# Shared PSUM banks, seven chained products for three input blocks, joint last-query scores, and an order written out by hand

## The chip, the core and the metric

The kernel runs on one core of a Trainium2 chip. Its time is the device time of one execution in microseconds (us). The engines are named as in the profile: PE does matrix products (PEld is its weight load), ACT applies functions, DVE does elementwise work, POOL starts loads, SP starts stores and transposing DMAs. PE writes its results to PSUM, eight banks of 128 partitions x 512 fp32 numbers; ACT and DVE read them there. Each engine runs its own queue in order and waits where a value isn't there yet.

## The reference

Attention with a relative position bias (8 batches, 8 heads, 576 positions, 64 numbers per head), and then two dense layers on its result:

```python
scores = scale * np.matmul(q, k.transpose(0, 1, 3, 2))
scores = scores + bias.transpose(2, 0, 1)[None, :, :, :]   # bias_table[bucket(|i - j|)]
attn = np.exp(scores - np.max(scores, axis=-1, keepdims=True))
attn = attn / (np.sum(attn, axis=-1, keepdims=True) + 1e-09)
out = np.matmul(attn, v)
...
x = np.ascontiguousarray(out.transpose(0, 2, 1, 3)).reshape(B * S, H * D)   # 4608 x 512
h = x @ w_in                                                                # 512 x 2048
g = np.maximum(0.01 * h, h)
return (g @ w_out).astype(np.float32)                                       # 2048 x 512
```

## The kernel before

**Attention.** The 8 heads of a batch make four pairs; `n` counts the 32 pairs. For a pair, q and k are loaded (POOL), copied next to each other by DVE (`rows`, buffer `pr`, three of them), transposed by a DMA on SP's queue (`turn_by_dma`, buffer `tu`) and copied into `qt` and `kt` (`take_turned`). The scores of a pair are six units: u = 0 to 3 are 128 keys each against queries 0 to 511, one product for each head, which stand in the two halves of PE's rows (64x128 tiles) and run at the same time; u = 4 is queries 512 to 575 (the "last queries") of both heads against 4 x 128 keys, with `apart` having put the two heads' queries side by side with zeros between, in the full 128x128 tile; u = 5 is the last 64 keys. ACT takes the exponent of each (`expo`), DVE multiplies the five blocks by the bias's exponent (`band`), PE multiplies by v (`av`, `av_tail`), whose 65th column gives the sum, DVE divides head by head (`norm`), and the result is transposed into `xT` by a DMA (`x_dma`).

**Dense layers.** 512 positions make a tile T, of which there are nine. `ffn_in` makes 16 blocks h of 128 x 512, each from four products of 512 columns (L556), ACT applies the leaky ReLU (`ffn_act`, L560). The second layer is done with seven block products in place of eight (`product`, L604): DVE makes four sums of blocks of g first (`mix_g`, L582), each product has its own PSUM bank, and DVE adds the seven up in `y` (`combine`, L617). `mix_weights` makes the sums of weights once.

**PSUM.** The eight banks are shared out by use: two double banks for scores (S), one bank (O), three banks (M) for everything else.

**Order.** Nothing is scheduled by the compiler. Class `Plan` lists all steps with an estimated cost, what they come after and what PSUM they take, and makes each engine's queue by a list scheduler with ranks, shifted by a table (`SHIFT`, `HOLD`, `SWAP`). Where it expects PE to be idle in the first 26 us it puts in filling products (`spin`, L879). The first layer can't start before the first batch's attention is done, since all four pairs make up the 512 columns of x; from then on the products of the dense layers stand between the attention steps, and after the last pair they run alone.

Of the kernel before, what the change touches and what calls it, by code (L numbers as in the profile page):

```python
# [36 lines left out]
class Plan:  # L37


    LAG, COLD, WARM, EARLY, PATIENCE = 0.25, 4.9, 26.0, 34.0, 0.3  # L40

    SHIFT = {
# [12 lines left out]
    }  # L55

    HOLD = {
        2: 19.6, 15: 64.2, 20: 6.9, 31: 13.4, 33: 28.9, 38: 9.6, 40: 11.1, 43: 25.5, 208: 57, 1127: 179.7,
    }

    SWAP = (62, 63, 88, 91, 117, 184, 212, 261, 269, 270, 952, 1141,)

    def __init__(self, slots):
        self.tasks = []
        self.slots = {k: [0.0] * v for k, v in slots.items()}
        self.slots["M"][-1] = self.WARM

    def add(self, engine, cost, after, go, rank, take=(), give=(), tail=0.0, at=None):
        t = {"engine": engine, "cost": cost, "after": list(after), "go": go, "rank": rank, "n": len(self.tasks),
             "take": list(take), "give": list(give), "tail": tail, "end": at, "start": at}  # L70
        if at is None:
            self.tasks.append(t)
        return t

    def link(self, ins):

        for t in self.tasks:
            t["after"] = [ins[d[1:]] if isinstance(d, tuple) else d for d in t["after"]]
            t["behind"] = [d for d in t["after"] if d["engine"] == t["engine"] == "POOL"]
            t["after"] = [d for d in t["after"] if not any(d is o for o in t["behind"])]  # L80

    def order(self):

        for t in self.tasks:
            t["rank"] += self.SHIFT.get(t["n"], 0)
            if t["n"] in self.SWAP:
                t["engine"], t["cost"] = t["other"]
        free, done, waiting, ring = {}, [], {}, 0.0
        slots = {k: list(v) for k, v in self.slots.items()}
        for t in self.tasks:  # L90
            waiting.setdefault(t["engine"], []).append(t)
        while any(waiting.values()):
            best = None
            for e, ts in waiting.items():
                now = free.get(e, 0.0)
                ready = []
                for t in ts:
# [5 lines left out]
                    for k in set(t["take"]):  # L103
                        s, m = sorted(self.slots[k]), t["take"].count(k)
                        r = max(r, s[m - 1]) if len(s) >= m else None
                        if r is None:
                            break
# [53 lines left out]
def kernel(  # L161
# [10 lines left out]
    nc = tc.nc  # L172
# [741 lines left out]
```

## Time and profile before

| | us |
|---|---|
| time, three runs | 367.48, 367.71, 370.26 (median 367.71) |
| profiled execution: its span, first to last instruction | 367.0 |
| PE busy | 355.8 |
| DVE busy | 266.8 |
| ACT busy | 246.5 |
| first product of the dense layers starts (L556) | 33.13 |
| last product ends | 362.09 |

The profile holds the span of its execution alone; the median of the runs is 0.7 us above it, which is what this text takes for what lies around a span. A product's row in the trace lasts longer than the engine is taken by it, since products overlap: what PE can do is read from the starts of products that follow each other. A row with "x8" is eight instructions, from the first's start to the last's end. The chain of waits names, from the last instruction backwards, what each step waited for. The idle time before an instruction is put down to what ended it.

### The profile page before, as it was taken

What the parts mean: (1) busy time and instruction counts of PE and PEld (TensorE: products, weight loads), DVE (VectorE), ACT (ScalarE), POOL (GpSimd) and SP (SyncE); (2) the same over time, 40 slices, a digit from 0 to 9 for tenths busy, and PEclk for the clock granted to TensorE, in tenths of its full rate; (3) what the DMA queues carried; (4) which work ended last, traced back from release to release, by engine and by line L of the source; (5) the groups of instructions that cost most, each with busy time, mean ns of one, the idle gap of its engine ahead of it and who ended that gap; (6) DMA issues with size and microseconds to landing.
All of it is one profiled execution on the core that took longest, in us unless ns stands there. A gap on an engine that the chain in (4) does not pass through costs nothing.

```text
span 367.0 us, 9617 instructions
## 1 busy us (share of the span) xinstructions
PE 355.8 (97%) x4022; PEld 239.7 (65%) x4022; DVE 266.8 (73%) x650; ACT 246.5 (67%) x356; POOL 71.8 (20%) x107
## 2 busy tenths in 40 slices
PE   8999999799999999999999999999999999999994
PEld 6666556575587556865678788656875587445883
DVE  6997799598799679975997779757984384320482
ACT  5998998558955897579857885797568911565000
POOL 8955122082007100700052005000000000000000
PEclk9999999999999999999999999999999999999999
DMA  8999999999919993999189929932222110300033
GB/s 128 153 182 196 204 180 154 134 81 191 215 20 89 192 162 73 118 205 170 20 86 197 156 71 89 116 53 72 82 21 75 20 59 2 114 0 2 1 116 114
DMA packets 103163, 39.56 MB, mean 108 GB/s; under 512 B 83152, under 2 KB 97488, under 8 KB 103120
## 3 DMA queue, kind: packets, MB, share of 16 engines
q0 software_dynamic: 53424, 18.21, 48.5%
q1 hardware_dynamic: 49488, 20.46, 30.6%
q8 instruction: 31, 0.51, 0.6%
q10 hardware_dynamic: 208, 0.29, 0.3%
q14 instruction: 12, 0.10, 0.1%
HBM read 36.70 MB, written 9.44 MB: 126 GB/s over the span
## 4 chain that ended last, share of the span: by engine, by line
PE 87%; DVE 5%; ACT 3%; DMA 3%; issue 1%; ACTq 0%
PE pm L556 32%; PE pm L604 28%; PE ps_s L437 8%; PE ps_om L506 5%; PE ps_o L506 5%; DMA tu<-pr 3%; ACT at L451 2%; PE ps_s L441 2%; PE ps_s L444 2%; PE ps_w L879 2%; DVE at L471 1%; PE ps_o L491 1%; DVE sum L582 1%; PE ps_tx L533 1%; DVE opair L519 0%
## 5 line engine op out<-in xcount | busy, mean ns | idle before, releaser
L451 ACT ACTIVATE at<-ps_s 128x1024 bf16<-128x1024 f32 x124 | 121.0, 1027 | 27.4 <-PE ps_s L437 27.3
L556 PE MATMUL pm<-xT,w_in_sb 128*128 128x512 bf16 (+1 forms) x640 | 134.1, 358 | 0.0
L560 ACT ACTIVATE gt<-pm 128x512 bf16<-128x512 f32 x144 | 84.7, 604 | 50.1 <-PE pm L556 48.4
L556 PEld LDWEIGHTS <-w_in_sb 128*128 128x128 bf16 x640 | 59.1, 98 | 57.1 <-issue 5.1
L471 DVE TENSOR_TENSOR at<-at,hk 128x768 bf16<-128x768 bf16 (+4 forms) x156 | 67.1, 448 | 30.6 <-ACT at L451 22.6
L604 PEld LDWEIGHTS <-gt 128*128 128x128 bf16 x576 | 54.6, 98 | 10.8 <-issue 3.6
L249 POOL DMA_DIRECT2D vn<-in_v_dram x32 | 30.2, 954 | 145.2 <-PE ps_o L506 130.0
L617 DVE TENSOR_TENSOR y<-pm,y 128x512 f32<-128x512 f32 (+1 forms) x54 | 41.9, 775 | 20.8 <-PE pm L604 19.3
L604 PEld LDWEIGHTS <-sum 128*128 128x128 bf16 x432 | 41.3, 98 | 9.6 <-issue 2.5
L506 PEld LDWEIGHTS <-at 128*128 128x128 bf16 x1240 | 41.1, 98 | 4.0 <-issue 1.2
L437 PE MATMUL ps_s<-qt,kt 64*128 64x512 bf16 x256 | 40.3, 382 | 1.3 <-ACT at L453 0.7
L604 PE MATMUL pm<-w_out_sb,sum 128*128 128x256 bf16 x288 | 35.4, 273 | 0.0
L604 PE MATMUL pm<-mix,gt 128*128 128x256 bf16 x288 | 34.8, 273 | 0.0
L604 PE MATMUL pm<-w_out_sb,gt 128*128 128x256 bf16 x288 | 33.9, 273 | 0.0
L453 ACT ACTIVATE at<-ps_s 128x512 bf16<-128x512 f32 x31 | 18.6, 601 | 13.2 <-PE ps_s L441 13.2
L506 PE MATMUL ps_o<-vn,at 128*128 128x65 bf16 x640 | 25.5, 193 | 0.8 <-issue 0.7
L506 PE MATMUL ps_om<-vn,at 128*128 128x65 bf16 x600 | 24.1, 195 | 0.8 <-DVE at L471 0.8
L437 PEld LDWEIGHTS <-kt 64*128 64x128 bf16 x256 | 8.5, 94 | 19.4 <-issue 17.7
L458 ACT ACTIVATE at<-ps_s 128x576 bf16<-128x576 f32 x31 | 20.3, 656 | 0.0
L582 DVE TENSOR_TENSOR sum<-gt 128x1024 bf16<-128x1024 bf16 x18 | 12.3, 688 | 11.1 <-ACT gt L560 11.0
L604 PE MATMUL pm<-mix,sum 128*128 128x256 bf16 x144 | 17.7, 273 | 0.0
L519 DVE TENSOR_TENSOR opair<-ps_o,rcp 128x320 bf16<-128x320 f32 (+2 forms) x34 | 16.4, 481 | 1.2
(96 smaller groups left out, 346.1 us busy)
## 6 DMA issues: line engine op xcount, KB each, us to landing
out_dram<-y SPq DMA_DIRECT2D x18, 512.0 KB, 3.4
vn<-in_v_dram POOLq DMA_DIRECT2D x32, 128.0 KB, 6.3
qn<-in_q_dram POOLq DMA_DIRECT2D x14, 288.0 KB, 10.8
kn<-in_k_dram POOLq DMA_DIRECT2D x14, 288.0 KB, 11.2
w_in_sb<-in_moe_w_in_dram POOLq DMA_DIRECT2D x2, 1024.0 KB, 11.3
w_out_sb<-in_moe_w_out_dram POOLq DMA_DIRECT2D x2, 1024.0 KB, 18.1
qn<-in_q_dram POOLq DMA_DIRECT2D x4, 144.0 KB, 4.3
v<-in_v_dram POOLq DMA_DIRECT2D x16, 32.0 KB, 6.9
```

What stands on the lines that cost most here:

```text
L249: nc.gpsimd.dma_start(out=vn[i][:, c, :, 0:D], in_=v[b, :, c * P : (c + 1) * P, :].rearrange("h s d -> s h d"),)
L437: nc.tensor.matmul(ps[:, e, :], lhsT=kt[r, u * P : (u + 1) * P], rhs=qt[r, 0:512], start=True, stop=True)
L451: nc.scalar.activation(at[:, :, u, 0:512], ps, AF.Exp, scale=scale)
L453: nc.scalar.activation(at[:, :, :, 512:S].rearrange("p e c i -> p c e i"), ps[:, 0, :].rearrange("p (c e i) -> p c e i", e=2, i=SL), AF.Ex ...
L458: nc.scalar.activation(at4[:, 0:S], ps.rearrange("p e i -> p (e i)")[:, 0:S], AF.Exp, scale=scale)
L471: nc.vector.tensor_tensor(out=o, in0=o, in1=m, op=ALU.mult)
L506: nc.tensor.matmul(ps[:, ic, :], lhsT=at[:, o : o + P], rhs=vn[i][:, c, 2 * p + e, :], start=whole and c == 0, stop=not whole and ic == NJ ...
L519: nc.vector.tensor_tensor(out=opairs[n][:, lo:hi, e * D : (e + 1) * D], in0=ps[:, lo:hi, 0:D], in1=rcp.to_broadcast([P, hi - lo, D]), op=A ...
L556: nc.tensor.matmul(pms[T, f][:, o : o + n], lhsT=w_in_sb[:, c, f * P : (f + 1) * P], rhs=xT[c][:, x : x + n], start=(c == 0 and i == 0), s ...
L560: nc.scalar.activation(gts[T][:, f, :], pms.pop((T, f)), AF.Prelu, bias=0.0, scale=1.0, alpha=0.01)
L604: nc.tensor.matmul(ps[:, ts, :], lhsT=l[:, ts * P : (ts + 1) * P], rhs=r, start=ts == 0 and j == 0, stop=ts == 1 and j == NK - 1)
L617: nc.vector.tensor_tensor(out=out_, in0=ps, in1=x, op=ALU.add)
```

## The change

- **PSUM.** One pool of four double banks replaces the three. A planner's rule (`choose`) picks a free bank or double for each use when the order is replayed.
- **Scores.** From pair 4 on, pairs are taken two by two (`plan_two`). The last queries of two pairs share one double bank (`score_last`): 16 products of 64 columns in 64x128 tiles, the two heads at the same time, with two `expo_last` behind them. `apart` is no longer needed for q there. The units of scores are single (before: two by two), and stand in another order.
- **Division.** Both heads' outputs stand in one double bank and are divided together (`norm_both`).
- **First layer of T = 6, 7, 8.** Seven block products in place of eight, in four units u of 512 columns of h (`in_product`, 4 products of 256 columns each). They are chained: products 1, 6, 7 and 4 add up in one bank X, and after the first three the sum so far is copied out (`in_take`); 2 stands in its own bank, 5 and 3 add up in Y. DVE adds the copies (`in_add`), ACT applies the ReLU to the results (`in_act`). `mix_x` and, once, `mix_w_in` make the sums of blocks.
- **Second layer.** The same chain: `out_take` copies after products 1, 6, 7 and 4, `out_add` adds three times. `mix_g` writes over blocks of g; two of its four sums are made in one piece. In the last tile the last product's two halves have a bank and a store each.
- **Buffers.** `pr` has two buffers (before: three). `take_turned` reads in order and writes with a stride of six elements (before: the other way round).
- **Order.** Each engine's queue is a written list of step numbers (`QUEUES`); ranks and shifts are gone.

```diff
-    LAG, COLD, WARM, EARLY, PATIENCE = 0.25, 4.9, 26.0, 34.0, 0.3
-    SHIFT = {
-        36: 486.5, 43: 362.5, 60: 11.5, 66: -54.5, 68: -313, 81: 1183.5, 119: -494.5, 126: -591.5, 150: 46, 176:
...
+    LAG, COLD, WARM, TURN = 0.25, 4.9, 26.0, 0.095
+    QUEUES = {
...
+        "ACT": """
+            16 1 20 19 42 40 62 38 67 71 48 91 46 77 75 44 73 69 100 106 102 98 125 157 127 96 104 133 129 131 164 135
...
-    NPR, NTU = 3, 3
+    NPR, NTU = 2, 3
...
-    ps_s_pool = ctx.enter_context(tc.tile_pool(name="ps_s", bufs=2, space=bass.MemoryType.PSUM))
-    ps_o_pool = ctx.enter_context(tc.tile_pool(name="ps_o", bufs=1, space=bass.MemoryType.PSUM))
-    ps_m_pool = ctx.enter_context(tc.tile_pool(name="ps_m", bufs=3, space=bass.MemoryType.PSUM))
+    ps_pool = ctx.enter_context(tc.tile_pool(name="ps", bufs=1, space=bass.MemoryType.PSUM))
+    doubles = [ps_pool.tile([P, 2, 512], FP32, name=f"ps{i}") for i in range(4)]
...
-            src = turned[n][:, j * NC : (j + 1) * NC, :].rearrange("p c r -> p r c")
+            src = turned[n % NTU][:, j * NC : (j + 1) * NC, :]
...
-        copy(out=t[:, 0:S].rearrange("p (r c) -> p r c", c=NC), in_=src)
+        copy(out=t[:, 0:S].rearrange("p (r c) -> p c r", c=NC), in_=src)
...
+    def score_last(n):
+        ps = double(("s", n, NJ))
+        for i in range(2):
+            qt, kt = qts_[(n + i) % NQT], kts_[(n + i) % NQT]
+            for c in range(NJ):
+                o = (i * NJ + c) * SL
+                for e in range(2):
+                    r = slice(e * D, (e + 1) * D)
+                    nc.tensor.matmul(ps[:, e, o : o + SL], lhsT=kt[r, c * P : (c + 1) * P], rhs=qt[r, 512:S],
+                                     start=i == 0 and c == 0, stop=i == 1 and c == NJ - 1)
...
+    def norm_both(n):
+        ps = double(("o", n))[:, :, 0 : (NJ + 1) * (D + 1)].rearrange("p e (i d) -> p e i d", d=D + 1)
+        rcp = rc_pool.tile([P, 2, NJ + 1, 1], FP32, name="rcp2")
+        nc.vector.reciprocal(rcp, ps[:, :, :, D : D + 1])
+        nc.vector.tensor_tensor(out=opairs[n % NOP].rearrange("p i (e d) -> p e i d", e=2), in0=ps[:, :, :, 0:D],
+                                in1=rcp.to_broadcast([P, 2, NJ + 1, D]), op=ALU.mult)
...
+    def in_product(T, u, k):
+        key, first = {1: ("X", True), 6: ("X", False), 7: ("X", False), 4: ("X", False),
+                      2: ("Z", True), 5: ("Y", True), 3: ("Y", False)}[k]
+        ps = bank((key, T, u)).rearrange("p (j t) -> p j t", j=2)
+        for j in range(2):
+            m = slice(j * P, (j + 1) * P)
+            for c in range(KH):
+                l, r = {
+                    1: lambda: (w_in_blocks[:, 0, c, u, 0, m], x_block(T, 0, 0)[:, c]),
...
+                }[k]()
+                nc.tensor.matmul(ps[:, j, :], lhsT=l, rhs=r, start=first and j == 0 and c == 0,
+                                 stop=k in (2, 4, 3) and j == 1 and c == KH - 1, skip_group_check=True)
...
+    def in_take(T, u, s, key, copy):
+        ps = bank((key, T, u)).rearrange("p (j t) -> p j t", j=2)
+        copy(out=stage[u % 2][:, s], in_=ps)
...
+    CHAIN = {1: "a", 6: "a", 7: "a", 4: "a", 2: "b", 5: "c", 3: "c"}
...
+    SEVEN = 6
...
+        prod(1, 0, of(0, 0, NK, 0), [A])
+        c11 = take(0, ps[1] + was.get((0, 0), []))
+        sm[1] = add("DVE", 1.13, ps[1] + [sm[k, lo] for k in (0, 2) for lo in (0, NK // 2)], lambda: mix_g(1, 0, NK), 1)
...
+        prod(6, 2, [c11, sm[1]])
+        c12 = take(1, ps[6] + was.get((0, 1), []))
...
+        prod(7, 4, [c12, sm[2, 0], sm[2, NK // 2]])
+        c22 = take(3, ps[7] + was.get((1, 1), []))
+        prod(4, 5, [c22])
```

How the queues moved is shown at three places. On PE, the last queries' scores of a pair in the steady part and what follows them, before (`ps_s` is the scores' double bank, `kt` and `qt` the turned keys and queries, `pm` a bank of the second layer):

```order
L441 LDWEIGHTS kt_113
L441 MATMUL ps_s<-qt,kt_113 128x128
L444 LDWEIGHTS kt_113
L444 MATMUL ps_s<-qt,kt_113 128x512
L445 LDWEIGHTS kt_113
L445 MATMUL ps_s<-qt,kt_113 128x64
L604 LDWEIGHTS sum_98
L604 MATMUL pm_1610<-w_out_sb,sum_98 128x256
```

and on PE after the change, at the end of such a block of two pairs (L517 is the block, L497 a unit u < 4, L740 the second layer):

```order
L517 LDWEIGHTS kt_93
L517 MATMUL ps_67<-qt_96,kt_93 128x64
L497 LDWEIGHTS kt_92
L497 MATMUL ps_68<-qt_95,kt_92 128x512
L497 LDWEIGHTS kt_92
L497 MATMUL ps_68<-qt_95,kt_92 128x512
L740 LDWEIGHTS g
L740 MATMUL ps_66<-w_out_sb,g 128x256
```

Four products of 128 columns for each pair, which stood with u = 5 and the dense layers in the full tile, have become sixteen of 64 columns for two pairs, which stand with the units u < 4 in the 64-row tile. On DVE, the end of the program before (`gt` is g, `sum` its sums, `pm` a product's bank):

```order
L612 COPY y<-pm_5875 128x2x256
L582 TENSOR_TENSOR gt<-gt 128x4x256
L582 TENSOR_TENSOR sum_100<-gt,sum_99 128x1024
L617 TENSOR_TENSOR y<-pm_5896,y 128x2x256
L582 TENSOR_TENSOR sum_100<-gt,sum_99 128x1024
L617 TENSOR_TENSOR y<-pm_5916,y 128x2x256
L617 TENSOR_TENSOR y<-pm_5936,y 128x2x256
L617 TENSOR_TENSOR y<-pm_5954,y 128x2x256
L617 TENSOR_TENSOR y<-pm_5972,y 128x4x256
L617 TENSOR_TENSOR y<-pm_5990,y 128x2x256
```

and the end of DVE's queue now (`stage` holds the copies of the first layer's chains, `gs` a sum of g):

```order
L686 TENSOR_TENSOR stage_80<-ps_67,stage_80 128x512
L712 TENSOR_TENSOR gs<-g 128x1024
L712 TENSOR_TENSOR g<-g 128x4x256
L712 TENSOR_TENSOR gs<-g 128x1024
L712 TENSOR_TENSOR g<-g 128x4x256
L712 TENSOR_TENSOR g<-gs,g 128x8x256
L712 TENSOR_TENSOR g<-g 128x8x256
L753 TENSOR_TENSOR y<-ps_67,y 128x2x256
L753 TENSOR_TENSOR y<-ps_66,y 128x256 x4
```

The additions to `y` that were spread over the last products are three (the last two in halves), and all sums of g, two of them twice as long, stand in a row behind the last addition of the first layer. On ACT, the last part of the queue before held nothing but the ReLU:

```order
L560 ACTIVATE gt<-pm_5710 128x512
L560 ACTIVATE gt<-pm_5716 128x512
L560 ACTIVATE gt<-pm_5722 128x512
L560 ACTIVATE gt<-pm_5728 128x512
L560 ACTIVATE gt<-pm_5848 128x512
```

and now it holds the copies of both layers' chains (`stage` the first layer's, `y` the second's) between the ReLUs:

```order
L748 COPY y<-ps_68 128x2x256
L681 COPY stage_80<-ps_69 128x512
L748 COPY y<-ps_68 128x2x256
L681 COPY stage_81<-ps_69 128x512
L748 COPY y<-ps_68 128x2x256
L681 COPY stage_80<-ps_69 128x512
L617 ACTIVATE g<-stage_81 128x2x256 x2
L617 ACTIVATE g<-stage_80 128x2x256
L617 ACTIVATE g<-stage_81 128x2x256
```

The next product of a chain on PE waits for the copy before it.

More of the change, by code (lines that the diff above doesn't have):

```diff
@@ L133, in place @@
-    def place(self, t, r, free, slots, ring):
-        e = t["engine"]
-        cost = t["cost"] * (1.8 if e == "PE" and r < self.COLD else 1.0)
-        t["start"], t["end"] = r, r + cost + t["tail"]
-        if "turns" in t:
-            t["end"] = max(r + 4.5, min(ring + 2.0, r + 11.0))
-        if "moves" in t:
-            t["end"] = ring = max(ring, r + t["cost"] + 1.0) + t["moves"]
-        t["idle"] = r - free.get(e, 0.0)
-        free[e] = r + cost
-        for k in t["take"]:
-            slots[k].remove(min(slots[k]))
-        for k in t["give"]:
-            slots[k].append(t["end"] + self.LAG)
-        return ring
+    @staticmethod
@@ L430, in score @@
     def score(n, u):
-        qt, kt = qts[n], kts[n]
-        ps = scores[n, u] = ps_s_pool.tile([P, 2, 512], FP32, name="ps_s")
+        qt, kt = qts_[n % NQT], kts_[n % NQT]
+        ps = double(("s", n, u))
         if u < NJ:
@@ L862 @@
+    prods = {}
     for n in range(N):
```

741 lines of the change are left out of this document (460 added, 281 removed), and 71 rows, old and new, of tables (QUEUES, SHIFT).

## The prediction

> **What bounds the kernel now.** I read the page's busy times, the stretches of 20 us, the PE's waits, and then the starts of products that follow each other.
>
> ```profile
> span 367.0 us, 9617 instructions
> PE 355.8 (97%) x4022; PEld 239.7 (65%) x4022; DVE 266.8 (73%) x650; ACT 246.5 (67%) x356; POOL 71.8 (20%) x107
> PEclk9999999999999999999999999999999999999999
> ```
>
> PE is the bound, at full clock. In the stretches (length, then busy us with the number of instructions for PE, PEld, DVE, ACT, POOL, then clock, DMA share and GB/s), PE is short of 20.00 up to 80 us only:
>
> ```profile
> 20.00:40.00 20.00, 19.22 (x320) 12.87 (x318) 16.83 (x54) 17.51 (x26) 9.60 (x14) 1.00 1.48 192
> 40.00:60.00 20.00, 18.92 (x211) 10.87 (x211) 17.99 (x41) 18.39 (x27) 5.45 (x8) 1.00 1.72 176
> 60.00:80.00 20.00, 17.52 (x234) 13.15 (x233) 15.66 (x41) 11.19 (x16) 5.25 (x5) 1.00 1.04 118
> 80.00:100.00 20.00, 20.00 (x201) 10.81 (x200) 16.50 (x47) 17.71 (x27) 5.11 (x7) 1.00 1.36 200
> ```
>
> The PE's own waits (what waited for what: us, times, longest), without the first, on a memset before any work:
>
> ```profile
> PE ps_om L491 <- DVE y L617: 1.7, 1, 1.7
> ...
> PE ps_om L506 <- DVE at L471: 0.8, 1, 0.8
> PE ps_o L506 <- issue: 0.7, 1, 0.7
> PE ps_s L437 <- ACT at L453: 0.7, 1, 0.7
> PE ps_s L444 <- ACT at L451: 0.2, 1, 0.2
> PE ps_s L437 <- ACT at L451: 0.2, 1, 0.2
> ```
>
> That is 4.3 us, all before 75 us. What a product takes from PE is in the chain of waits (start, us, what) and in PE's order of time (start, us, instruction):
>
> ```profile
> 314.32 22.45 PE pm L556 x104
> 336.76 10.48 PE pm L604 x96
> ```
>
> ```profile
> 37.80 0.39 PE L441 MATMUL ps_s<-qt,kt 128*128 128x128 bf16 x4
> 38.02 0.38 PE L444 MATMUL ps_s<-qt,kt 128*128 128x512 bf16 x1
> 38.24 0.19 PE L445 MATMUL ps_s<-qt,kt 128*128 128x64 bf16 x1
> 38.26 1.89 PE L556 MATMUL pm<-xT,w_in_sb 128*128 128x512 bf16 x8
> 40.09 0.61 PE L437 MATMUL ps_s<-qt,kt 64*128 64x512 bf16 x4
> 40.63 0.61 PE L556 MATMUL pm<-xT,w_in_sb 128*128 128x512 bf16 x2
> ```
>
> A product of 512 columns takes 22.45 / 104 = 0.216 us, one of 256 takes 10.48 / 96 = 0.109, one of 128 takes 0.22 / 4 = 0.055. L445's 64 columns take 0.02 to 0.03. Eight of 512 should end 1.73 after 38.26, at 39.99; the 64-row products begin at 40.09: changing the tile's form costs 0.10. Back again likewise: two pairs of 0.22 from 40.09 end at 40.53, the next starts at 40.63. Two products in the two halves of the rows run as one:
>
> ```profile
> 100.98 0.19 PE L491 MATMUL ps_o<-v,at 64*128 64x65 bf16 x1
> ...
> 101.11 0.19 PE L491 MATMUL ps_om<-v,at 64*128 64x65 bf16 x1
> 101.23 0.78 PE L506 MATMUL ps_om<-vn,at 128*128 128x65 bf16 x20
> ```
>
> Five such pairs and one change of form take 0.25 us, so a pair of 65 columns takes 0.03.
>
> **The change part by part: PE's work.**
>
> *First layer.* Removed: 3 tiles x 16 blocks x 4 products of 512 = 192 x 0.216 = 41.5 us. Added: 3 tiles x 4 units x 7 products x 4 matmuls of 256 = 336 x 0.109 = 36.6. **-4.9 us**, all on the path: PE has no wait after 75 us. The Trainium skill, TensorE: Matmul & The Clock Gate, section "Back-to-back issue gap", speaks against this edit: in a stream of weight load and product it gives 131 ns for 512 columns and 81 ns for 128, so that halving a product saves less than half. By it (an estimate: 98 ns for 256, in between) the edit would remove 25.2 and add 32.9, +7.8 us. The rows above are such a stream, and 256 columns take half of what 512 take; the sum goes by them.
>
> *Last queries.* Removed: 28 pairs x 4 x 0.055 = 6.2. Added: 14 blocks of 8 products in each half of the rows, 112 pairs of 64 columns at 0.03 = 3.2. Bounds: 112 x 0.02 = 2.2 by L445, or as much as now, 6.2, if 64 rows don't overlap at this width; the row of 65 columns is so near that I take it. **-3.0.**
>
> *Changes of form.* PE's two orders hold 151 and 167 neighbours with different forms, 16 x 0.096 = **+1.5** (bounds: 0.09 to 0.10 for one). The block needs the 64-row form, the product it replaces stood with u = 5 in the full one.
>
> *Second layer, first layer of T = 0 to 5, the other scores, `av`*: the same products, 0. The filling products (38 before, 33 now) lie in idle time, 0.
>
> **The change part by part: waits.** The costs of the other engines (line, engine, what, count; busy us and mean ns of one; idle before):
>
> ```profile
> L451 ACT ACTIVATE at<-ps_s 128x1024 bf16<-128x1024 f32 x124 | 121.0, 1027 | 27.4 <-PE ps_s L437 27.3
> L617 DVE TENSOR_TENSOR y<-pm,y 128x512 f32<-128x512 f32 x45 | 30.9, 686 | 12.8 <-PE pm L604 11.3 <-DMA out_dram<-y 1.1
> L519 DVE TENSOR_TENSOR opair<-ps_o,rcp 128x320 bf16<-128x320 f32 x32 | 15.7, 491 | 1.1
> L582 DVE TENSOR_TENSOR sum<-gt 128x1024 bf16<-128x1024 bf16 x18 | 12.3, 688 | 11.1 <-ACT gt L560 11.0
> L612 ACT COPY y<-pm 128x512 f32<-128x512 f32 x2 | 1.2, 586 | 1.0 <-PE pm L604 1.0
> L416 DVE TENSOR_TENSOR qt<-qt,own 128x128 bf16<-128x128 bf16 x32 | 6.8, 216 | 0.6 <-ACT qt L412 0.6
> L412 DVE COPY kt<-tu 128x576 bf16<-128x576 bf16 x24 | 16.2, 674 | 0.0
> L381 DVE COPY pr<-qn 96x768 bf16<-96x768 bf16 x27 | 10.0, 370 | 4.2 <-DMA tu<-pr 4.2
> ```
>
> DVE loses 28 `apart` (6 us) and half of the steps of 28 divisions, and has 38 steps on `y` where it had 61 (27 copies out are ACT's now; 38 us less in all, by the rows above with about 0.3 us, an estimate, for the reciprocal and the fixed part that a joint division saves); it gains 36 `in_add`, 10 copies (46 x 0.686 = 32 us), `mix_x` and `mix_w_in` (about 10): four more than it loses, and late, where the stretches show room:
>
> ```profile
> 320.00:340.00 20.00, 20.00 (x110) 10.57 (x109) 3.48 (x6) 12.08 (x21) 0.00 (x0) 1.00 0.00 1
> ```
>
> ACT gains 53 - 2 copies of 0.586 = 30 us in all, to some 277 of 360. Neither becomes the bound over the whole. `take_turned`'s stride is on the writing side now; no row shows such a write. Bounds for one: the 0.37 us of a copy that is plain on both sides (L381), or twice the 0.67 of L412; the second would be 47 x 0.67 = 31 us more on DVE, which its idle time takes after 80 us and not before. I take no change, the row of the same count of elements with the stride on the other side.
>
> *The first 80 us.* PE starts with fillers and waits for exponents (ACT 17.51 and 18.39 of 20 above). Of the 4.3 us of waits, 1.1 are for scores' banks (the three `ps_s` rows), which four shared doubles relieve; 2.5 (`ps_om`) come from one late transpose:
>
> ```profile
> DVE pr L381 <- DMA tu<-pr: 4.2, 1, 4.2
> DMA to landing us min/median/max: 3.3/7.2/15.8
> ```
>
> (The first row is a wait, as above; the second the transposes' time from issue to landing.) DVE stood 4.2 us for a free `pr`, and PE behind it. The new order takes the early pairs sooner, so ACT's exponents bind harder there, and two `pr` in place of three make such a wait possible again. Bounds: -4.3 (all gone) to +4 (one more such wait and 1.5 us of ACT). I take half of the waits: **-2.0**.
>
> *The chains.* How long a copy keeps PE, from the first layer's rhythm and a score that waits for ACT:
>
> ```profile
> 307.22 1.89 PE L556 MATMUL pm<-xT,w_in_sb 128*128 128x512 bf16 x8
> 308.28 0.60 ACT L560 ACTIVATE gt<-pm 128x512 bf16<-128x512 f32 x1 [13.42 <-PE pm L556]
> ```
>
> The first four products are issued by 307.22 + 0.86 = 308.08 and ACT starts at 308.28: 0.20, then 0.586, then some 0.05 to the next product: 0.84 us. Between a product and the next of its chain PE has, at the tightest places, 8 products of 256 columns (half a second-layer product, or two `in_product`): 0.87 us. So a chain is just covered where ACT is free at that moment. What is left: at the seam from T = 8's first layer to its second, product 6 waits for 0.20 + `in_add` 0.69 + ReLU 0.60 + two sums of 0.69 + a double sum of about 1.3 and five handovers of 0.05 = 4.4 us, behind which 4 x 0.87 = 3.5 of products stand: 0.9. And ACT's queue isn't always free: 7 copies have a cover of 0.87 and 6 more one of at most 1.2, counted along PE's order; at 0.085 on average, 1.1. **+2.0**; bounds 0 (nothing queued, a shorter sum) and 6 (0.4 at each of 13, plus 0.9).
>
> *The end.*
>
> ```profile
> 358.43 3.66 PE L604 MATMUL pm<-w_out_sb,sum 128*128 128x256 bf16 x32
> 362.12 0.69 DVE L617 TENSOR_TENSOR y<-pm,y 128x512 f32<-128x512 f32 x1 [0.52 <-PE pm L604]
> ```
>
> After the last product 4.9 us remain to 367.0: 0.69, a store of 512 KB and the finish. Half the addition (0.4) and a store of 128 KB: **-0.7**, between 0 and -1.5.
>
> Sum: 367.0 - 4.9 - 3.0 + 1.5 - 2.0 + 2.0 - 0.7 = 359.9. The median of the runs lies 0.7 above this span: **360.6 us**.
>
> **The rivals.**
>
> *A, the chains stall.* There are 12 units x 3 and 9 tiles x 3 copies, 63 places where PE waits for one that ACT or DVE must reach in its queue. For it: an exponent of 1.03 us ahead of a copy leaves a cover of 0.87 short by 1.0; ACT is busy 11.19 to 18.39 of 20 in the stretches above. Against: the other covers are 1.3 us and more. At w per place the time is 358.6 + 63 w: no gain from w = 0.14, slower by 1% from 0.20. At a quarter of the places behind an exponent, w = 0.25: **374 us**. Chance 0.08, about half of it slower by over 1%.
>
> *B, late transposes.* Two `pr` let DVE stand for a transpose once a batch (latency up to 15.8 us above, when loads run), with all `band` and divisions queued behind. Each such time cost PE 2.5 us. Against: the row shows one in 24 transposes. Two to three more: 360.6 + 5 to 7.5 = **367 us**. Chance 0.12.
>
> *C, the waits vanish.* All 4.3 us go, the chains cost only the 0.9: 360.6 - 2.3 - 1.1 = **357 us** or, with the end's full 1.5, 356. Chance 0.12.
>
> *D, weight loads show.* Each half-width product has a load of its own:
>
> ```profile
> L604 PEld LDWEIGHTS <-gt 128*128 128x128 bf16 x576 | 54.6, 98 | 10.8 <-issue 3.6
> ```
>
> 98 ns hide behind a product of 109, with 11 to spare. If the first layer's loads, from blocks of `w_in` and of its sums, took 0.04 more, 336 products would cost 13.4 more: **374 us**; from 0.123 for a product on, the edit is worth nothing. (The skill's page above would make it 360.6 + 4.9 + 7.8 = 373.) Against: the second layer's products have the same form and lose nothing. Chance 0.02.
>
> *E, the 64-column block doesn't overlap* and the form costs more: +3 and the like, **363.5**. Chance 0.05.
>
> **How the numbers follow.** Forecast (358.5 to 363): 0.61. What a measurement tells from no change is about 1%, 3.7 us, so faster is below 364.0: forecast, C and E, 0.78. Within 1%: B and half of A, 0.16. Slower: the rest of A, and D, 0.06. The range takes C below and the middle of B above: 356 to 366.5, with A, D and the top of B outside.
>
> **What would show it.** Right: 256-column products of L676 at 0.109 us, the L517 block at 8 x 0.03, PE waits of 5 to 7 us with those after 250 us in front of L676 and L740, the last product some 4.2 us before the end. Wrong: L676 slower than half of L556; waits of PE for copies (`stage`, `y`) in each tile (A); DVE standing before `pr` (B); PE short of 20.00 in a stretch between 80 and 280 us.

## The result, and the profile after

The changed kernel takes 425.61 us (median of four runs, 423.93 to 428.85) where the kernel before takes 368.99 beside it (367.48 to 372.81): 1.153 times as long, 95% interval 1.143 to 1.1635. The forecast was 360.6 with a range up to 366.5, so it missed by 65 us and on the wrong side: the prediction gave "slower" a chance of 0.06, and the slowest of its rivals was 374 us. The profiled execution took 424.66 us. The kernel before was run again beside each group of runs below, with medians of 368.85 to 371.98 us; a difference of two times from different groups is therefore good to some 3 us, and the ratios are each to the kernel before of the same group.

The page of the changed kernel, its span, busy times, granted clock and chain of waits:

```profile
span 422.9 us, 10035 instructions
...
PE 366.7 (87%) x4253; PEld 257.4 (61%) x4273; DVE 295.7 (70%) x588; ACT 288.7 (68%) x410; POOL 76.2 (18%) x107
...
PEclk9759699999999999996999999999999999999999
...
PE 60%; ACT 17%; DVE 11%; DMA 5%; issue 3%; SPq 2%; DVEq 0%; ACTq 0%
```

PE was busy 97% of the span and is now busy 87%; ACT and DVE have come into the chain; and the clock, full all through before, is not granted in two places. The stretches of 20 us (columns as in the prediction):

```profile
20.00:40.00 20.00, 14.41 (x171) 8.49 (x173) 15.26 (x32) 13.95 (x16) 7.72 (x11) 0.67 1.46 193
40.00:60.00 20.00, 14.41 (x208) 9.72 (x209) 12.69 (x37) 15.63 (x16) 3.33 (x4) 0.83 0.84 123
...
180.00:200.00 20.00, 14.58 (x163) 10.00 (x160) 11.51 (x20) 8.83 (x11) 0.75 (x2) 0.84 1.07 152
...
280.00:300.00 20.00, 17.37 (x164) 9.55 (x165) 12.12 (x23) 11.69 (x18) 0.00 (x0) 1.00 0.18 34
...
380.00:400.00 20.00, 18.60 (x166) 15.97 (x165) 14.34 (x20) 9.56 (x18) 0.00 (x0) 1.00 0.14 53
```

There is a hole at the start, one at 180 us, and a steady loss everywhere else, even after 280 us, where few transfers are under way (34 and 53 GB/s) and, of 20 us, ACT has 8 and more to spare and DVE 5.7 and more.

To size the losses I add up, over the trace, the interval from one PE start to the next, and take off what each instruction takes where PE does not wait (0.216, 0.109, 0.055 and 0.03 us and the change of form, as in the prediction). What PE has to do by that sum fell from 348.1 to 341.0 us, 7.1 less: the 4.9 + 3.0 - 1.5 of the forecast and 0.5 of fillers. What it loses rose from 12.7 to 76.1 us. (The trace lacks the records of some 20 products, so such sums are good to about 2 us.) That is the whole result, and the runs below show that it has two causes.

PE's longest waits that name an engine, from the list of all waits of the changed kernel (what waited for what: us, times, longest):

```profile
PE ps L628 <- ACT g L617: 5.8, 11, 0.9
...
PE ps L497 <- ACT qt L472: 5.4, 2, 2.8
...
PE ps L628 <- DVE opair L595: 5.0, 1, 5.0
...
PE ps L740 <- DVE y L753: 3.9, 7, 0.9
...
PE ps L740 <- ACT y L748: 3.2, 6, 0.7
...
PE ps L676 <- DVE stage L686: 2.3, 4, 0.9
```

L472 is the copy `take_turned`, L617 the ReLU, L748 and L753 copy and addition of the second layer's chains, L686 the addition of the first layer's. Most of the waits are short, 0.9 us at the most, with two kinds of long ones: for `take_turned`, and one for a division (L595).

### The profile page after: what moved, and what is told of

It is laid out like the page before. It is cut to its first block, busy times and chain, and to the rows that moved or that the text cites. A ratio compares the mean times of both kernels' runs of the same rounds, so it can differ in the third digit from the quotient of the medians.

```text
span 422.9 us, 10035 instructions
## 1 busy us (share of the span) xinstructions
PE 366.7 (87%) x4253; PEld 257.4 (61%) x4273; DVE 295.7 (70%) x588; ACT 288.7 (68%) x410; POOL 76.2 (18%) x107
## 4 chain that ended last, share of the span: by engine, by line
PE 60%; ACT 17%; DVE 11%; DMA 5%; issue 3%; SPq 2%; DVEq 0%; ACTq 0%
PE ps L740 19%; PE ps L628 18%; PE ps L577 7%; ACT g L617 6%; PE ps L676 5%; PE ps L497 5%; DMA xT<-opair 4%; ACT qt L472 3%; ACT at L524 2%; ACT kt L472 2%; DVE stage L686 2%; DVE kt L472 2%; DVE y L753 2%; ACT stage L681 1%; PE ps L1201 1%
## 5 line engine op out<-in xcount | busy, mean ns | idle before, releaser
L524 ACT ACTIVATE at<-ps 128x1024 bf16<-128x1024 f32 x124 | 123.5, 1034 | 25.2 <-PE ps L497 23.6
L628 PE MATMUL ps<-xT,w_in_sb 128*128 128x512 bf16 (+1 forms) x430 | 90.7, 349 | 13.4 <-ACT g L617 5.8
L740 PEld LDWEIGHTS <-g 128*128 128x128 bf16 x864 | 82.6, 98 | 29.3 <-issue 16.7
L617 ACT ACTIVATE g<-ps 128x512 bf16<-128x512 f32 x108 | 61.5, 602 | 26.5 <-PE ps L628 20.4
L628 PEld LDWEIGHTS <-w_in_sb 128*128 128x128 bf16 x448 | 41.9, 98 | 50.0 <-issue 19.5
L740 PE MATMUL ps<-mix,g 128*128 128x256 bf16 x432 | 54.7, 275 | 6.4 <-DVE y L753 3.9
L740 PE MATMUL ps<-w_out_sb,g 128*128 128x256 bf16 x432 | 53.5, 273 | 2.8 <-DVE stage L686 1.3
L497 PE MATMUL ps<-qt,kt 64*128 64x512 bf16 x256 | 44.0, 399 | 8.4 <-ACT qt L472 5.4
L577 PE MATMUL ps<-vn,at 128*128 128x65 bf16 x1240 | 46.0, 194 | 3.0 <-ACT kt L472 1.6
L748 ACT COPY y<-ps 128x512 f32<-128x512 f32 x27 | 16.1, 595 | 34.8 <-PE ps L740 23.1
L686 DVE TENSOR_TENSOR stage<-ps,stage 128x512 f32<-128x512 f32 x36 | 24.4, 689 | 14.3 <-PE ps L676 6.4
L753 DVE TENSOR_TENSOR y<-ps,y 128x512 f32<-128x512 f32 (+1 forms) x29 | 18.7, 650 | 20.1 <-PE ps L740 13.3
L472 DVE COPY kt<-tu 128x576 bf16<-128x576 bf16 x24 | 27.6, 1149 | 2.8 <-PE ps L517 2.8
L497 PEld LDWEIGHTS <-kt 64*128 64x128 bf16 x256 | 10.4, 94 | 28.7 <-issue 24.4
L472 DVE COPY qt<-tu 128x576 bf16<-128x576 bf16 x23 | 26.1, 1136 | 0.0
L595 DVE TENSOR_TENSOR opair<-ps,rcp 128x640 bf16<-128x640 f32 x28 | 23.1, 825 | 3.6 <-DMA xT<-opair 2.6
L712 DVE TENSOR_TENSOR g<-g 128x1024 bf16<-128x1024 bf16 (+1 forms) x27 | 23.3, 868 | 3.1 <-PE ps L740 2.9
L617 ACT ACTIVATE g<-stage 128x512 bf16<-128x512 f32 x36 | 20.6, 628 | 4.0 <-PE ps L740 2.1
## 6 DMA issues: line engine op xcount, KB each, us to landing
w_in_sb<-in_moe_w_in_dram POOLq DMA_DIRECT2D x2, 1024.0 KB, 10.8
```

Of the source, the lines that this page charges most:

```text
L472: copy(out=t[:, 0:S].rearrange("p (r c) -> p c r", c=NC), in_=src)
L497: nc.tensor.matmul(ps[:, e, :], lhsT=kt[r, u * P : (u + 1) * P], rhs=qt[r, 0:512], start=True, stop=True)
L524: nc.scalar.activation(at[:, :, u, 0:512], ps, AF.Exp, scale=scale)
L577: nc.tensor.matmul(ps[:, ic, :], lhsT=at[:, o : o + P], rhs=vn[i][:, c, 2 * p + e, :], start=whole and c == 0, stop=not whole and ic == NJ ...
L617: nc.scalar.activation(out_, in_, AF.Prelu, bias=0.0, scale=1.0, alpha=0.01)
L628: nc.tensor.matmul(bank(("in", T, f))[:, o : o + n], lhsT=w_in_sb[:, c, f * P : (f + 1) * P], rhs=xT[:, c, x : x + n], start=(c == 0 and i ...
```

## Experiments

### The stride on the writing side

`take_turned` in the trace of the kernel before, then in that of the changed one (duration in ns: shortest, median, longest; first and last start):

```profile
L412 DVE COPY kt<-tu x24: 633/646/944, 53.4 to 269.9; 128x576 bf16<-128x576 bf16 x24
...
L412 DVE COPY qt<-ps_t x5: 741/758/759, 10.8 to 42.0; 128x576 bf16<-128x576 bf16 x5
L412 ACT COPY kt<-ps_t x4: 639/657/682, 6.6 to 63.8; 128x576 bf16<-128x576 bf16 x4
```

```profile
L472 DVE COPY kt<-tu x24: 1119/1130/1284, 74.5 to 317.2; 128x576 bf16<-128x576 bf16 x24
...
L472 ACT COPY qt<-ps x6: 2065/2084/2284, 10.2 to 88.5; 128x576 bf16<-128x576 bf16 x6
...
L472 DVE COPY kt<-ps x4: 2067/2080/2087, 14.9 to 62.5; 128x576 bf16<-128x576 bf16 x4
```

Same elements, same work; only the side that strides differs. A copy from a transposed load takes 1.13 us instead of 0.65, one from PSUM 2.08 instead of 0.76 on DVE and 0.66 on ACT. There are 16 of these from PSUM in the changed kernel, ten on ACT and six on DVE. The planner's costs for them still say 0.57, 0.72 and 0.53 us. Three runs take the stride apart: undone in the changed kernel, undone there for the copies from PSUM alone, and put alone into the kernel before.

```diff
-            src = turned[n % NTU][:, j * NC : (j + 1) * NC, :]
+            src = turned[n % NTU][:, j * NC : (j + 1) * NC, :].rearrange("p c r -> p r c")
         else:
-            src = bank(("t", n, j)).bitcast(BF16)[:, 0:S].rearrange("p (c r) -> p c r", c=NC)
+            src = bank(("t", n, j)).bitcast(BF16)[:, 0:S].rearrange("p (c r) -> p r c", c=NC)
         t = (qts_, kts_)[j][n % NQT]
-        copy(out=t[:, 0:S].rearrange("p (r c) -> p c r", c=NC), in_=src)
+        copy(out=t[:, 0:S].rearrange("p (r c) -> p r c", c=NC), in_=src)
```

> The changed kernel with one thing undone: the copies that follow the transposes write contiguously again and read with the stride. Theory 1 (the stride on the writing side is the cause): in the profile of the changed kernel such a copy takes 1.13 us from a transposed load and 2.07 to 2.09 us from PSUM, where 0.65, 0.75 and 0.65 stood before; with them back, PE's idle time falls from 76 us to about the 12 of the kernel before, and with 341 us of products the time is 358 to 366 us. Theory 2 (the chains and the fixed order are the cause): only what is lost before 200 us can come back; PE goes on losing 2 to 3 us in each 20 us after 240 us, where few such copies lie, and the time stays over 385 us. In between, 366 to 385: both, and the losses after 320 us, where there are no such copies at all (12 us in the profile), tell the chains' share.

> The stride goes back to the reading side for the 17 copies from PSUM alone, all before 91 us; the 47 copies of transposed loads keep writing with it (1.13 us each). Theory 1, early part: 16 copies x 1.35 us on ACT and DVE at the start, with PE idle and its clock down, cost most of the 30 us lost in the first 60 us; the time falls by about 22, to 403 us. Theory 1, late part: the 47 copies on DVE at 0.48 us more (23 us) are what keeps PE waiting all through; the time falls by less than 10. Theory 2: less than 10 as well, but then the run with all copies undone falls by no more.

> The kernel before with this one part of the change put in: its copies write with the stride. Theory 1: the 16 copies at the start and the 47 later ones cost it time too: it becomes slower by 10 to 25 us, 378 to 393 us, most of it before 80 us, where ACT and DVE are needed at once. Theory 2 (the order without slack makes the loss, and a copy as such is hidden): within 2% of the kernel before, up to 375 us.

Measured: all undone, 400.82 us (ratio to the kernel before 1.082, 1.075 to 1.0885); undone for PSUM alone, 402.31; put into the kernel before, 384.59 (ratio 1.037, 1.030 to 1.044). So the stride costs the changed kernel 24.8 us, of which 23.3 are the copies from PSUM at the start and only 1.5, which is within the noise, those from the transposed loads; and it costs the kernel before 3.7% too. Theory 1 holds for the start: the 402.31 is the 403 that its early part gave. But 400.8 is not its 358 to 366. It is over the 385 that Theory 2 gave, and as that theory had it, the losses late in the trace stay: behind the last of these copies PE loses 12.2 us in the changed kernel and 12.2 with the copies undone. In all PE still loses 52.1 us in that run, 12.6 of them before 60 us, 7.4 in one stall at 167 us, and 32 spread over all the rest. Whether the chains themselves do that, as Theory 2 says, or something else keeps PE waiting for a fraction of a microsecond at a time, at 40 to 60 places, these three runs do not tell.

### Whose product does a copy wait for?

At the start of the second layer of the last tile (T = 8) PE's order is product 1 for both halves of the rows, 16 instructions, then product 2 for one half, 8 more, in another bank. The copy L748 needs product 1. In the changed kernel's order of time (start, us, instruction, and in brackets its wait):

```profile
403.91 2.78 PE L740 MATMUL ps<-w_out_sb,g 128*128 128x256 bf16 x24 [1.14 <-DVE stage L686]
...
406.73 0.59 ACT L748 COPY y<-ps 128x512 f32<-128x512 f32 x1 [1.63 <-PE ps L740]
...
410.76 0.58 ACT L748 COPY y<-ps 128x512 f32<-128x512 f32 x1 [3.45 <-PE ps L740]
...
411.40 0.81 PE L740 MATMUL ps<-mix,g 128*128 128x256 bf16 x6 [0.67 <-ACT y L748]
```

Product 1 is through after 16 x 0.109 at 405.65; with the 0.20 us that the prediction found between a product and ACT's start, the copy could begin at 405.85, and ACT had been idle since 405.10. It begins at 406.73 = 403.91 + 24 x 0.109 + 0.20. It has waited for product 2 as well, which it does not read. The eight products that were to cover the copy are through before it starts.

The reason is in the kernel's program, not in the chip: a double of two banks is one tile (the piece of memory that the kernel asks for under one name), and the framework that sets the semaphores orders every two instructions of different engines that touch one PSUM tile, in whichever bank. Read off the compiled program, some 90 waits of ACT and DVE on PE count products of another bank than their own (about 15 of the 36 copies out of the second layer, about 33 of the 144 ReLUs); in the kernel before, whose single banks were tiles of their own, there are nine at the most, by one small instruction each. And the planner prefers, for a single bank, the one whose neighbour will be busy longest.

The next run changes the waits alone. After the program is written, two instructions of different engines that share no bank (and no cell of another tensor that either writes) are declared independent; the waits within a bank stay. Order, banks and work are unchanged. (`touched` lists the cells that an instruction reads or writes, and `meet` tells whether two lists overlap, in PSUM by bank.)

```diff
     plan.run(spin)
+    ps_names = {d.tensor.name for d in doubles}
...
+    seen = {}
+    for x in nc.cur_bb.bb.instructions:
+        at = touched(x)
+        for name in ps_names & at.keys():
+            for y, other in seen.get(name, [])[-400:]:
+                if y.engine != x.engine and not any(meet(at, other, k) for k in at):
+                    tc.declare_no_dep(x, y, reason="another bank")
+            seen.setdefault(name, []).append((x, at))
```

> Copies read with the stride again, and beside that the waits between engines on PSUM are made by single bank: where two instructions touch different banks of one double, neither waits for the other any more. Nothing else moves: order, banks and work are the same. Theory 3 (false waits: the doubles are one tile each, and an instruction on one bank waits for the work queued before it on the other): of the 52 us that PE lost in the run with the copies undone, the losses after 40 us other than the one of 5.5 us behind a division, some 33 us, mostly go: 366 to 374 us. Theory 2 (each chain's own latency and busy queues of ACT and DVE): PE's waits stay in front of the products; not below 392 us. In between: both.

> The changed kernel with the waits by single bank alone; its copies keep writing with the stride. If the two causes add up: 425.6 less what the waits by bank give beside the other copies (theory 3: 27 to 35 us), 390 to 399 us. If slow copies and false waits feed each other (a late copy holds both banks of a double), it falls by more, to 375 to 390. Theory 2: over 415 us.

Measured: 366.90 us with the copies read by stride (ratio 0.989, 0.981 to 0.996), 383.98 with them written by stride. The two causes in one table, in us:

| | waits by double | waits by bank | difference |
|---|---|---|---|
| copies write with the stride | 425.61 | 383.98 | 41.6 |
| copies read with the stride | 400.82 | 366.90 | 33.9 |
| difference | 24.8 | 17.1 | |

Theory 3 holds: 366.90 lies in its 366 to 374, the 12.2 us behind the last copy of the transposes fall to 2.2, and the chains' own latency, Theory 2, would have left at least 392. The causes feed each other by some 8 us (41.6 less 33.9, from groups of runs that are themselves good to a few us; 383.98 is in the 375 to 390 that was expected for that case). That a slow copy which holds a bank holds its neighbour with it is the likely way; no run shows it by itself. The same place with the waits by bank:

```profile
348.13 2.78 PE L740 MATMUL ps<-w_out_sb,g 128*128 128x256 bf16 x24
...
350.08 0.59 ACT L748 COPY y<-ps 128x512 f32<-128x512 f32 x1
...
353.13 1.92 PE L740 MATMUL ps<-mix,g 128*128 128x256 bf16 x16 [1.34 <-DVE g L712]
```

The copy starts at 348.13 + 16 x 0.109 + 0.20 = 350.07, as it should. What PE loses over the trace falls from 52.1 to 19.7 us, of which 8.3 are one stall, and these are the longest waits that are left on PE after the first 20 us (L595 is the division, L712 the mixing of the second layer):

```profile
PE ps L628 <- DVE opair L595: 5.9, 1, 5.9
PE ps L740 <- DVE g L712: 1.3, 1, 1.3
...
PE ps L497 <- DVE opair L595: 0.7, 1, 0.7
```

### The one stall that is left

The order of time around it, with the waits by bank and the copies read by stride:

```profile
156.31 0.36 DVE L445 COPY pr<-qn 96x768 bf16<-96x768 bf16 x1 [6.95 <-DMA tu<-pr]
156.59 0.21 DVE L476 TENSOR_TENSOR kt<-kt,own 128x128 bf16<-128x128 bf16 x1
156.72 1.22 DVE L712 TENSOR_TENSOR g<-g 128x2048 bf16<-128x2048 bf16 x1
157.86 0.21 DVE L594 RECIPROCAL rcp<-ps 128x10 f32<-128x10 f32 x1
159.76 0.82 DVE L595 TENSOR_TENSOR opair<-ps,rcp 128x640 bf16<-128x640 f32 x1 [1.69 <-DMA xT<-opair]
...
160.63 1.86 PE L628 MATMUL ps<-xT,w_in_sb 128*128 128x512 bf16 x4 [5.92 <-DVE opair L595]
```

DVE stood 6.95 us for one of the two `pr`, then 1.69 for an output buffer; PE's next bank was held until the division (L595) behind both. SP had issued what both waited for in one group, between 141 and 155 us (start, us of issuing):

```profile
141.37 3.81 SPq L449 DMA_TRANSPOSE tu<-pr  x2
145.23 1.71 SPq L762 DMA_DIRECT2D out_dram<-y  x1
146.99 8.10 SPq L601 DMA_TRANSPOSE xT<-opair  x2
```

and from 137.4 us on the load of `v` for batch 5 and of q and k for batch 6 were issued. These five took 7.5 to 13.3 us from issue to landing; five of the same kinds that SP issued from 124 to 129 us, when no load was being issued, took 2.7 to 3.7. In the kernel before, transposes issued between 114 and 124 us took 8.3 to 15.8 us, and PE did not wait there: the late landing is not new; that it holds PE up is. Whether that comes of the two `pr` in place of three or of the new order, no run tells. Three runs move steps in the written order, nothing else: one DVE copy three places later, two transposed stores earlier on SP, or both.

```diff
-... 451 614 608 1071 509 478 663 ...
+... 451 509 478 614 608 1071 663 ...
-... 545 661 559 1116 563 662 ...
+... 545 559 1116 563 661 662 ...
```

> The run with the copies read by stride and waits by bank, with one step moved in DVE's order: the copy into the q half of the transposes' buffer for pair 22, which stood 7.0 us for a free one of the two buffers, now stands behind the fourth mixing of tile 2's second layer and the joint division of pair 17. Theory 4a (two buffers: the standing copy holds up the division behind it, and that PE's bank): the stall of 6 us and the 2 us of slow clock behind it go, 359 us. Theory 4b (the division waits anyway, for an output buffer whose transposed store landed only at 159.7 us): no change, 365 to 368 us.

> As before, with a move in SP's order alone: the transposed stores of pairs 15 and 14 ahead of the transposes of pairs 21 and 20 and of a store of the output, behind which they stood from 131.9 and 138.4 to 147 and 152 us. Theory 4a: the copy still stands for its buffer until the transpose of pair 20 has landed (156.3, or somewhat earlier with less queued with it): 363 to 367 us. Theory 4b (the stores' place on SP sets it): the division of pair 17 follows at once when DVE gets to it; as DVE still stands for the buffer until about 155, 2 to 4 us are won, 363 to 365.

> Both moves. Theory 4a and 4b together (the copy for the buffer and the store each hold the division up): division at about 150 us, the stall of 8 us and its slow clock gone: 358 to 360 us. If the time stays at 364 or more, the stall has another cause (the transposes' own time beside the loads of v).

Measured: 367.99, 368.49 and 367.36 us, ratios 0.998, 0.9965 and 0.995, all the same as without the moves. The copy later gives the 365 to 368 of Theory 4b, the stores first give more than either theory allowed, and both together lie above the 364 that was to mean another cause. Each move did what it says, and another wait took over. The waits in the three runs, the copy later first, then the stores first, then both (in the last two the lines have numbers lower by one):

```profile
DVE opair L595 <- DMA xT<-opair: 8.5, 1, 8.5
PE ps L628 <- DVE opair L595: 7.2, 1, 7.2
```

```profile
DVE pr L444 <- DMA tu<-pr: 9.1, 1, 9.1
...
PE ps L627 <- DVE opair L594: 6.4, 1, 6.4
```

```profile
ACT y L747 <- DMA out_dram<-y: 5.6, 1, 5.6
...
PE ps L739 <- ACT y L747: 5.0, 1, 5.0
```

For 358 to 360 with both moves I had counted two users of late transfers; there is a third, the copy that needs `y`, whose store is in the same group. So it is not one wait but one group of five transfers that lands late. Is it late by itself (Theory 6), or because of the loads (Theory 5)? Two runs leave loads out:

```diff
-lambda: [load_v_part(b, j) for j in range(3)]
+lambda: [load_v_part(b, j) for j in range(3)] if b != 5 else None
-lambda hh=hh: load_qk(b, 4 * hh, 4 * hh + 4)
+lambda hh=hh: load_qk(b, 4 * hh, 4 * hh + 4) if b != 6 else None
```

> Copies read with the stride and waits by bank, and the load of v for batch 5 (0.58 MB, issued from 137.4 to 142 us) left out: batch 5 uses the v of batch 3, so its rows of the output are another computation. Theory 5 (the transposes, the store and the transposed stores that SP issues between 141 and 155 us land late because they share the DMA engines with that burst of loads): the stall of 8 us at 154 us shrinks to under 2 us, 359 to 362 us. Theory 6 (they are late by themselves: five transfers in a row on one queue, each issue 1.3 to 5 us): no change, 365 to 368 us.

> As the run without the load of v for batch 5, and the loads of q and k for batch 6, which come right behind it (142 to 146 us, 1.15 MB), left out as well; batch 6 then uses the q and k of batch 4. Theory 5: if the first part of the burst is what counts, the same as without v alone; if the whole burst, 358 to 360 us here and 362 to 365 without v alone. Theory 6: no change, 365 to 368.

Measured: 366.00 us without `v` alone (ratio 0.993, 0.988 to 0.997), 360.89 without both (ratio 0.980, 0.975 to 0.985). By its time the first run is in the range of Theory 6, and the second just above that of Theory 5; the traces tell more. In the profile of the first PE loses 0.5 us between 140 and 180 us, but 5.9 between 100 and 140: the stall has moved to the burst of loads before, where PE waits 3.8 us for a transposed store. In the profile of the second the five transfers land in 2.7 to 5.2 us, and no wait of PE is over 1.3 us. By Theory 6 the second run would have stayed at 365 to 368, so it falls: the group is late because of the loads. That they meet on the DMA engines is the likely way, but no run tells it from another path that they share. That the first run moved a stall instead of removing it I had not foreseen, and why the burst before then hurts is open.

Two last runs leave nothing out. The first has both moves and issues the store of `y`, too, ahead of the two transposes; the second, in addition, lets the loads of q and k for batch 6 wait until the transpose of pair 20 has landed.

```diff
-... 451 509 478 614 608 1071 663 ...
+... 451 1071 509 478 614 608 663 ...
...
+            if b == 6:
+                tc.add_manual_dep(ld.ins, turns[20].ins.name,
+                                  mybir.DependencyInfo(mybir.DependencyClass.Sync, mybir.DependencyReason.DATA))
```

> Nothing left out: copies read with the stride, waits by bank, the two moves of pair 22's copy and of the transposed stores of pairs 15 and 14, and the store of tile 1's second half, too, ahead of the transposes of pairs 21 and 20 on SP, so that three of the five late transfers are issued before or at the start of the burst of loads. Theory 5 (each transfer that is issued inside the burst lands late and holds up its own user): the waits for the output's store and for the transposed stores go, that for the transposes of pairs 20 and 21 stays, 4 to 5 us on DVE, of which PE sees 0 to 3: 360 to 364 us. If the burst then delays still others by as much: 365 to 368.

> As the run with the store first, and the loads of q and k for batch 6 wait until the transpose of pair 20 has landed, so that they no longer compete with it. Theory 5: the transposes land earlier, no stall of PE over 2 us between 140 and 165 us: 358 to 362 us, unless the later loads now come too late for pair 24 (then a stall of DVE before the copy of pair 24, 363 to 368).

Measured: 364.61 us (ratio 0.984, 0.979 to 0.990) and 360.15 us (ratio 0.973, 0.968 to 0.978). The first lies just above its 360 to 364, with one wait of PE of 3.3 us left, for an addition to `y`; the second is in its 358 to 362. The last is the best version found, 2.7% faster than the kernel before, with all work done. Its span and the longest waits of PE (lines 4 higher than in the changed kernel):

```profile
span 357.9 us, 10039 instructions
...
PE ps L744 <- DVE g L716: 1.3, 1, 1.3
PE ps L632 <- DMA xT<-opair: 1.2, 1, 1.2
```

PE loses 11.2 us in it, 5.6 of them before 80 us, and no wait is longer than 1.3 us.

## Why the prediction was wrong, point by point

**The first layer, -4.9: right.** In the run with the waits by bank, whose chain of waits has PE at work without a break (start, us, what):

```profile
315.55 10.04 PE ps L676 x92
```

10.04 / 92 = 0.109 us for 256 columns. The rule of the Trainium skill, TensorE: Matmul & The Clock Gate, section "Back-to-back issue gap", by which the edit would have cost 7.8 us, does not describe this stream. Rival D falls with it.

**The last queries, -3.0: right.** In the same run's order of time, PE:

```profile
202.74 0.41 PE L517 MATMUL ps<-qt,kt 64*128 64x64 bf16 x16
202.98 0.38 PE L497 MATMUL ps<-qt,kt 64*128 64x512 bf16 x2
```

Eight pairs in 0.24 us, 0.03 each; the 64-row halves overlap at 64 columns. Rival E falls. With the changes of form PE's work came out at 341.0 us, 7.1 less than before, as summed.

**`take_turned`, "I take no change": wrong, the first of the two failed steps.** The row I chose, the same count of elements with the stride on the other side, was not near. The copies from transposed loads came inside the bounds (1.13, under twice 0.67), and that these would be hidden after 80 us was right: 1.5 us. The copies from PSUM I had not bounded apart: they take 2.08 us, outside the bounds, ACT has ten of them beside the DVE's six, and they lie where the prediction itself said that ACT is busy 17.51 and 18.39 of 20 us and that DVE has no idle time to take them. Cost: 24.8 us with the waits by double, 17.1 without. The row to ask for was the one of each source and each engine.

**The chains, "+2.0" with the cover "counted along PE's order": wrong, the second and larger one.** I counted which products stand between a product and the next of its chain, took them as cover, and so assumed that a copy waits only for its own bank. The change's first words, PSUM banks shared by all stages, say where to look: which tile does each bank belong to, and who else touches it? With that assumption made true, by the waits by bank, the sum nearly holds: after 180 us, where the chains of the first layer lie, PE loses 3.3 us in all, 1.3 of it at the seam of T = 8, where I had 0.9; 2.0 was the forecast for the chains of the whole span. With the waits as the change has them the kernel takes 33.9 us more; put on the 63 places of Rival A alone, that would be 0.54 each. Rival A had places (copies in front of L740 and L676) and the sign, but not the cause: ACT was idle 1.63 us before the copy shown above. It is not a full queue, it is a wait for the wrong product. And the ReLUs of the unchanged first layer (L617, in front of L628) suffer as well, which no rival had.

**The first 80 us, -2.0: hidden by both causes.** With them gone PE loses 7.4 us before 80 us (waits by bank) or 5.6 (the last run), against 10.8 before: -3.4 to -5.2, nearer to Rival C, and past the lower bound of -4.3 at its end.

**Rival B, late transposes with two `pr`: it is there,** once, and costs 8.3 us in the run with the waits by bank: 5.9 of waiting and the rest of slow clock. The prediction had 2.5 us for each such time, too little, because the whole group of transfers is late and not one transpose, and because of the clock.

**The end, -0.7: about right.** In the last run 4.4 us remain after the last product, where 4.9 did.

Of the wrong side as a whole: the forecast of 360.6 describes a kernel that the change nearly was. With the stride back, the waits by bank and the loads out of the way it is 360.15. That this is within 0.5 us of 360.6 is in part luck: its terms missed by up to 3 us, some up and some down, the moves in the order were not part of the change, and the kernel before took 371.53 us beside that run, not the 367.71 that the forecast started from.

## What to carry to other kernels

When a change merges buffers, ask of each wait which instruction it counts to: dependencies may be kept by tile, and a copy then waits for whatever PE has queued on the tile's other half, which eats exactly the products that were to cover it. Sharing that looks free in a plan of banks is free only if the waits are as fine as the plan. And when a layout turns over, price the copy for each source and each engine; a row with the stride on the other side is no bound.

## What was not expected of the hardware

A copy of 128 x 576 bf16 that writes with a step of 12 bytes takes 1.13 us on DVE from SBUF and 2.08 from PSUM, on ACT 2.08 from PSUM, where one that reads with a step of 192 bytes and writes plainly takes 0.65, 0.76 and 0.66. The Trainium skill, SBUF — State Buffer, has in its section "Door 1: The DMA port swizzle" a remark that each access that crosses into a new line of 16 bytes pays. Here both kinds cross at most of their elements, and the one that writes with the step is the slower one, 1.13 against 0.65, a difference that the remark does not make. Whether the reading side pays as well differs by engine. The kernel before has copies of this size from PSUM with no step on either side (line, engine, what, count; busy us and mean ns of one; idle before):

```profile
L538 ACT COPY xT<-ps_tx 128x576 bf16<-128x576 bf16 x3 | 1.9, 637 | 6.3 <-PE ps_tx L533 6.3
...
L538 DVE COPY xT<-ps_tx 128x576 bf16<-128x576 bf16 x4 | 1.8, 450 | 0.5 <-PE ps_tx L533 0.5
```

So on ACT a step in reading from PSUM cost nothing that shows (0.66 against 0.64) and on DVE it cost two thirds more (0.76 against 0.45), while a step in writing cost three times the plain copy and more on both.

The clock: in the stall at 154 us PE stood for 6 us, and the products after it were slow. In the stretches of 5 us of the run with the waits by bank (columns as above):

```profile
155.00:160.00 5.00, 0.00 (x0) 0.00 (x0) 2.00 (x5) 1.41 (x2) 0.00 (x0) 0.77 0.94 184
160.00:165.00 5.00, 4.37 (x19) 2.30 (x19) 2.82 (x6) 0.80 (x3) 0.00 (x0) 0.55 0.48 92
```

The four products of 512 columns at 160.63 shown above take 0.43 us each, twice 0.216. The Trainium skill, TensorE: Matmul & The Clock Gate, section "HAM oscillation — how this bites in real kernels", says that a wait longer than a window of some 3.4 us halves the clock for a while after; the trace of this run agrees. But a wait need not be that long: in the changed kernel the clock was 0.67 and 0.83 in the stretches from 20 to 60 us, and no wait of PE up to there is over 2.8 us. It was at half from 12.9 to 16.3 us and from 19.7 to 33.3, behind waits of 2.6 and 2.8 us for `take_turned`. So the slow copies cost time twice, by the wait and by the clock behind it.

The group of transfers that was issued inside a burst of loads was late as a group (7.5 to 13.3 us to land, against 2.7 to 3.7 for the same kinds issued without loads beside them); moving two of its members only handed the stall to the user of another.
